# Attention and a Fourier-mixing block on one core: values and scores of batch 1 become two steps, and the block sums are scaled one step ahead

## The chip, the cores and the metric

The kernel runs on 1 core of one Trainium2 chip. The metric is the device time of one execution in microseconds (us), lower is better. The engines of the core are named as in the profile: PE is TensorE (its weight loads are PEld), DVE is VectorE, ACT is ScalarE, POOL is GpSimd, and SP is SyncE, which issues nearly all transfers here. Each engine runs its own list of instructions in order; the lists are tied together by semaphores.

## The reference, cut to what matters

There are 4 batches, 8 heads, 768 tokens and a head size of 64. A query sees the tokens closer than 16 to it and, beside them, one summary for each block of 32 tokens: the maximum of the block's keys and the mean of its values.

```python
k_sum = k.reshape(B, H, nb, block, D).max(axis=3)        # block = 32, nb = 24
v_sum = v.reshape(B, H, nb, block, D).mean(axis=3)
scores_l = scale * q @ k^T, where |i - j| < 16, else -1e9
scores_s = scale * q @ k_sum^T + log(block)
a = softmax(concat(scores_l, scores_s));  attn = a @ concat(v, v_sum)
x = attn as (batch, 768, 512)
u = x + real(fft(fft(x, axis=1), axis=2))
un = (u - mean) / sqrt(var + 1e-6)                        # over the last axis
out = u + maximum(un @ w_ch1, 0) @ w_ch2                  # 512 -> 2048 -> 512, float32
```

## The kernel before, in words

The kernel is one program for all four batches. Heads go in pairs g = 0 to 3, so a batch has four attention steps of two heads each. The work of one batch runs beside that of another: while batch b does its dense products, batch b+1 does its attention.

**The attention of batches 1 to 3** (`gen_attention`) is made of these parts for each pair:

- `prepare` turns keys and queries (for batch 1 on PE, 12 transposes `qk`, copied by ACT at L709; for later batches on DVE) and takes the block maxima of the keys (`km`, DVE, L714).
- `scores` makes 48 small matmuls `sc` (L773: 64 rows of weights, 32 columns), an exponential on ACT (L779) and a mask on DVE (`p`, recorded at the helper's line L567).
- `sum_scores` makes 4 matmuls `ss` with the block maxima (L789) and one exponential.
- `values` first makes one matmul `vs` (L796) that picks the pair's block sums out of the tile `vbs`, and scales them by a mask of ones and zeros, `half_of`, into the single SBUF tile `vs`: for batch 1 with one DVE multiply (L801), for batches 2 and 3 with two ACT activations (L799). Then it makes 48 small matmuls `av` with the values' windows (L810), 6 matmuls `av` with `vs` (L815), and DVE takes the reciprocal of the sums (`rec`, L819) and writes the result to `x`.
- `load_values` fetches the windows of a later pair into one of two buffers `vw`.

All of `qk`, `sc`, `ss`, `vs` and `av` take their PSUM tiles from one pool of four, in the order in which the program asks for them.

**The dense work** of a batch is: the Fourier transform along the tokens (`y`, L1209) and along the features (`mx`), normalising, transposes `unt` (L1287), then `gen_hidden` (h tiles, `hx`, `hy`, `hz`, L1313, seven products of two matmuls for each of the hidden tiles j = 0 to 7, four per half) and `gen_out` (`o`, L1359, for the first half of batch 0, else L1382). For batch 0 the weights arrive as float64 and are converted tile by tile (`make`, `convert`): raw `words` are loaded by SP, DVE makes two steps (L1058, L1059), ACT two (L1060, L1061), DVE three more (L1063, L1065 and a product), and for each W1 tile and the later W2 tiles four sums follow. A list `plan` says which tile is converted from which stage on. So in the first 235 us DVE converts weights beside everything else.

**What sets the order.** Python generators are stepped in turn by `drive`. Batch 1's attention is stepped in two calls: first beside batch 0's Fourier work, `drive((gen_fourier(0), 4, 600), (first(weights, 66), 12, 0), (first(attn, 5), 1, 0))`, and then beside batch 0's hidden and output work, `drive((most, 5, 0), (weights, 15, 0), (attn, 1, 0))`: in each round five dense steps, fifteen weight steps and one attention step. For batch 1 a pair took two attention steps: one with `values` of pair g-1, `scores` and `sum_scores` of pair g, and `load_values`; one with `prepare` of the next pair and its loads. Batches 2 and 3 had three yields between values and scores already. Within this program order a scheduler moves instructions on each engine by planned durations and dependencies; the result, the order of instructions as built, is fixed before the kernel runs and can be read. In that order batch 1's scores of a pair followed the values of the pair before directly for pairs 2 and 3.

Of the kernel before, what the change touches and what calls it, by code (L numbers as in the profile page):

```python
# [490 lines left out]
def _main_program(ctx, tc, q, k, v, moe_w_ch1, moe_w_ch2, out):  # L491
# [51 lines left out]
    vw_bufs = [cpool.tile([P, nb, D1], FP, name=f"vw{i}") for i in range(2)]  # L543
# [14 lines left out]
    def abank(shape, name):  # L558
        return psum.tile(shape, FP, tag="attn", bufs=4, name=name)

    def bank(shape, name):
        return psum.tile(shape, FP, tag="bank", bufs=4, name=name)
# [3 lines left out]
    def tt(out, in0, in1, op):  # L566
        return nc.vector.tensor_tensor(out=out, in0=in0, in1=in1, op=op).ins  # L567
# [28 lines left out]
    def room(name):  # L596
        return bpool.tile([P, NC * 2 * S], FP, tag="room", name=name)
# [52 lines left out]
    def load_values(b, g):  # L650
        if is_wide(b):
            load_wide_values(b, g)
            return
        load_narrow_values(b, g)
# [30 lines left out]
    def prepare(b, g, *which):  # L685
        qn, kn = (nat[b, g, n] for n in range(2))
        kt, km = kt_bufs[g % 2], km_bufs[g % 2]
        qt = apool.tile([P, S], FP, tag="qt", name=f"qt_{b}_{g}") if 0 in (which or (0,)) else None
        for n in which or (1, 0):
            src, dst = (kn, kt[:, W:W + S]) if n else (qn, qt)  # L690
            if (b, g) > (2, 0):
                with tc.issue_after(marks["dense"]):
                    nc.vector.transpose(out=dst, in_=src.rearrange("p m c -> p (m c)"))
                continue
            if is_wide(b):
                for h in range(2):
                    ps = bank([P, S2], f"qk_{b}_{g}_{h}")
                    for s in range(HT):
                        for e in range(2):
                            nc.tensor.matmul(ps[D * e:D * (e + 1), s:S2:HT], src[:, e, h, s, :], ident, start=True, stop=True)  # L700
                    nc.scalar.copy(out=dst[:, S2 * h:S2 * (h + 1)], in_=ps)
            else:
                for e in range(2):

                    ps = abank([P, S2], f"qk_{b}_{g}_{e}")
                    for j in range(NST // 2):
                        nc.tensor.transpose(ps[:, P * j:P * (j + 1)], src[:, e, j, :], ident)
                    for s in range(2):
                        nc.scalar.copy(out=dst[D * e:D * (e + 1), s:S:2], in_=ps[D * s:D * (s + 1)])  # L709
        if which == (0,):  # L710
            nat[b, g] = qt
            return
        with tc.issue_after(marks["fold", 0]) if (b, g) == (1, 0) else ExitStack():
            nc.vector.tensor_reduce(out=km[:, 0:nb], in_=kt[:, W:W + S].rearrange("p (n f) -> p n f", f=BLOCK),  # L714
                                    op=ALU.max, axis=AX.X)
        nat[b, g] = qt
# [72 lines left out]
                nc.tensor.matmul(ps[r:r + 32, :], km[rows, :], qt[rows, S2 * h:S2 * (h + 1)], start=True, stop=True)  # L789
        nc.scalar.activation(out=p, in_=ps, func=AF.Exp, scale=SC)  # L790

    def values(b, g, p, pm, x):
        vw = vw_bufs[g % 2]
        ps = abank([P, D], f"vs_{b}_{g}")
        vb, pick = sums[b, g]
        nc.tensor.matmul(ps, pick, vb, start=True, stop=True)  # L796
        if b > 1:
            for r in range(2):
                nc.scalar.activation(out=vs[:, r, 0:D], in_=ps, func=AF.Identity, scale=half_of[:, r:r + 1])  # L799
        else:  # L800
            tt(vs[:, :, 0:D], ps[:, None, :].to_broadcast([P, 2, D]),  # L801
               half_of[:, :, None].to_broadcast([P, 2, D]), ALU.mult)

        av = [abank([P, NST, D1], f"av_{b}_{g}_{r}") for r in range(2)]
        for t in range(NST):
            h = t // HT
            for j in range(4):
                for r in range(2):
                    rows, i = slice(64 * r, 64 * (r + 1)), 4 * t + j
                    nc.tensor.matmul(av[r][32 * j:32 * (j + 1), t, :], p[rows, h, i - NB2 * h, :], vw[rows, i, :],  # L810
                                     start=(t == 0), stop=False, skip_group_check=True)
        for t in range(HT):
            for r in range(2):
                rows = slice(64 * r, 64 * (r + 1))
                nc.tensor.matmul(av[r][:, t:t + HT + 1:HT, :], pm[rows, P * t:P * (t + 1)], vs[rows],  # L815
                                 start=False, stop=(t == HT - 1), skip_group_check=True)
        for r in range(2):
            rc = rec[:, b * NP + g, r]
            nc.vector.reciprocal(out=rc, in_=av[r][:, :, D])  # L819
            xo = x[:, 0, P * g + D * r:P * g + D * (r + 1)]  # L820
            xo = bass.AP(xo.tensor, xo.offset, [list(xo.ap[0]), [HT * DM + D * (1 - 2 * r), 2], [DM, HT], [1, D]])
            tt(xo, av[r].rearrange("p (h t) d -> p h t d", h=2)[:, :, :, 0:D],
               rc.rearrange("p (h t) -> p h t", h=2)[:, :, :, None].to_broadcast([P, 2, HT, D]), ALU.mult)
# [3 lines left out]
    def following(b, g, n):  # L827
        i = b * NP + g + n
        return divmod(i, NP) if i < B * NP else None
# [129 lines left out]
    def gen_attention(b):  # L959
        x = bpool.tile([P, NST, DM], FP, tag="x", bufs=2, name=f"x_{b}")  # L960
        x_of[b] = x
        held = None
        if b == 2:
            load(2, 1)
            load(2, 2)
        if b > 1:
            yield
            yield
            with tc.issue_after(marks["load"]):
                block_sums(b, 0)  # L970
            for _ in range(2):
                yield
        for g in range(NP + 1):
            n1, n3 = (following(b, g, n) for n in (1, 3))
            if held:
                values(b, g - 1, *held, x)
                if n1 and b > 1:
                    load_values(*n1)
            if g == NP and b > 1:
                turn_tiles(b, x)  # L980
                for _ in range(17):
                    yield
                rooms[b] = room(f"fold_{b}")
                steps = fold_batch(b, split_fold(b, rooms[b]))
                while True:
                    with tc.issue_after(marks["dense"]):
                        done = next(steps, steps) is steps
                    if done:
                        break
                    yield  # L990
            elif held and b > 1:
                yield
                yield
                yield
            if g < NP:
                held = scores(b, g)
                sum_scores(b, g, held[1])
            if g and n1 and b == 1:
                load_values(*n1)
            if g == 1 and b > 1:  # L1000
                block_sums(b, 1)
            if g == NP and b > 1:
                return
            yield
            if g == NP:
                return
            if b > 1:
                yield
                yield
            if n1:  # L1010
                prepare(*n1, *((1,) if b > 1 else ()))
            if b > 1:
                yield
                yield
                if n1:
                    prepare(*n1, 0)
            if n3 and not (b == 1 and n3 > (2, 0)):
                load(*n3)
            yield
            if b > 1:  # L1020
                yield
# [431 lines left out]
    def drive(*gens):  # L1453


        gens = list(gens)
        rounds = max(g[1] for g in gens)
        while gens:
            for s in range(rounds):
                for g in list(gens):  # L1460
                    gen, n, ahead = g
                    for _ in range(n * (s + 1) // rounds - n * s // rounds):
                        with tc.high_priority(ahead) if ahead else ExitStack():
                            done = next(gen, gens) is gens
                        if done:
                            gens.remove(g)
                            break

    def first(gen, n):
        for _, step in zip(range(n), gen):  # L1470
            yield

    weights = gen_weights()
# [16 lines left out]
        yield from gen_attention(1)  # L1490

    attn = second_attention()
    drive((gen_fourier(0), 4, 600), (first(weights, 66), 12, 0), (first(attn, 5), 1, 0))
    block_sums(1, 1)
    for b in range(B):

# [66 lines left out]
```

## Time and profile before

| what | value |
| --- | --- |
| median of 5 runs | 803.88 us (800.92 to 807.67) |
| the profiled execution | 812.89 us, its span 810.7 us |
| mean granted PE clock in the span | 0.980 |
| PE busy | 786.2 us (97%), 5914 matmuls |
| DVE busy | 496.2 us (61%) |
| ACT busy | 229.3 us (28%) |
| POOL busy | 61.5 us (8%) |
| chain that ended last | PE 90%, DVE 5%, ACT 3%, issue 2% |

The span runs from the first to the last instruction; 2.2 us of the profiled execution lie outside it. The profiled execution was 9.0 us longer than the median. Busy shares are averages over the whole span. By stretches, DVE is much fuller early on: 44.6 of 55 us between 145 and 200 us, 32.0 of 36 us between 200 and 236 us. The clock column of the windows is the clock that PE was granted, 1.00 being full. "issue" stands for time in which an engine waited for nothing that the profile shows.

### The profile page before, as it was taken

How to read it: one execution, taken by the hardware profiler on the slowest of the kernel's cores; microseconds unless marked ns; L12 is line 12 of the kernel's file. 1: busy time of each engine (PE TensorE's matmuls, PEld its weight loads, DVE VectorE, ACT ScalarE, POOL GpSimd, SP SyncE). 2: the span in 40 equal slices, each digit the busy share in tenths (PEclk: the TensorE clock that was granted, in tenths of full speed). 3: DMA queues.
4: the chain of work that ended last, by engine and by line, in shares of the span. 5: the costliest groups of instructions: out<-in, count | busy, mean ns of one | idle time of the engine just before them, and what ended most of it. 6: DMA issues, size and time to landing. Idle time of an engine off the chain costs nothing.

```text
span 810.7 us, 14470 instructions
## 1 busy us (share of the span) xinstructions
PE 786.2 (97%) x5914; PEld 572.9 (71%) x5914; DVE 496.2 (61%) x1115; ACT 229.3 (28%) x509; POOL 61.5 (8%) x103
## 2 busy tenths in 40 slices
PE   9988989999999999999999999999999999999997
PEld 6786655545569875588659875688659875786586
DVE  5789678688998836573476826464476723532352
ACT  3544448442745212210116212210116102001200
POOL 0012030000000012200030002300030000000000
PEclk9989699999999999999999999999999999999999
DMA  9999568499584457996344049820514044206001
GB/s 218 205 282 200 100 216 239 149 237 288 174 263 132 106 167 170 253 151 134 129 176 153 27 142 209 215 75 27 226 40 153 27 170 155 91 0 228 0 27 55
DMA packets 133354, 121.83 MB, mean 150 GB/s; under 512 B 94464, under 2 KB 114912, under 8 KB 133088
## 3 DMA queue, kind: packets, MB, share of 16 engines
q1 hardware_dynamic: 132016, 118.53, 53.0%
q0 software_dynamic: 576, 2.10, 0.7%
q8 instruction: 48, 0.79, 0.4%
q10 hardware_dynamic: 688, 0.20, 0.1%
q14 instruction: 26, 0.21, 0.1%
HBM read 97.22 MB, written 23.59 MB: 149 GB/s over the span
## 4 chain that ended last, share of the span: by engine, by line
PE 90%; DVE 5%; ACT 3%; issue 2%; DMA 0%; POOL 0%; SPq 0%; POOLq 0%
PE hx L1313 20%; PE ox L1382 18%; PE hz L1313 9%; PE oz L1382 9%; PE o L1359 5%; PE hy L1313 5%; PE oy L1382 4%; PE y L1209 3%; PE sc L773 3%; PE mx L1168 2%; PE av L810 2%; PE av L815 1%; PE unt L1287 1%; DVE p L567 1%; PE ss L789 1%
## 5 line engine op out<-in xcount | busy, mean ns | idle before, releaser
L1313 PE MATMUL hx<-u,w 128*128 128x384 f32 x512 | 189.7, 499 | 1.3 <-DVE h L567 0.7
L1313 PEld LDWEIGHTS hx<-u,w 128*128 128x128 f32 x512 | 96.6, 193 | 72.8 <-DVE h L567 4.3
L1313 PE MATMUL hz<-u,w 128*128 128x384 f32 x256 | 93.3, 487 | 0.0
L1382 PE MATMUL oz<-w,s 128*128 128x256 f32 x336 | 81.1, 379 | 0.0
L1382 PE MATMUL ox<-w,s 128*128 128x256 f32 x336 | 80.3, 380 | 0.0
L1382 PE MATMUL ox<-w,h 128*128 128x256 f32 x336 | 79.8, 381 | 0.0
L567 DVE TENSOR_TENSOR x<-ox,x 128x256 f32<-128x256 f32 x84 | 35.3, 423 | 67.7 <-PE ox L1382 67.5
L1313 PEld LDWEIGHTS hz<-u,w 128*128 128x128 f32 x256 | 48.8, 191 | 34.7 <-issue 0.8
L1382 PEld LDWEIGHTS ox<-w,h 128*128 128x128 f32 x336 | 63.0, 190 | 11.1 <-issue 1.2
L1382 PEld LDWEIGHTS ox<-w,s 128*128 128x128 f32 x336 | 63.0, 190 | 9.3 <-DVE x L567 0.8
L1382 PEld LDWEIGHTS oz<-w,s 128*128 128x128 f32 x336 | 63.4, 190 | 8.5
L1324 ACT COPY h<-hx 128x384 f32<-128x384 f32 x32 | 15.3, 479 | 189.7 <-PE hx L1313 189.7
L567 DVE TENSOR_TENSOR h<-hy,h 128x384 f32<-128x384 f32 x32 | 17.8, 558 | 48.6 <-PE hy L1313 48.5
L1313 PE MATMUL hy<-u,w 128*128 128x384 f32 x128 | 47.5, 493 | 0.0
L567 DVE TENSOR_TENSOR h<-hx,h 128x384 f32<-128x384 f32 x32 | 17.8, 556 | 45.5 <-PE hx L1313 45.5
L1359 PE MATMUL o<-w,h 128*128 128x512 f32 x96 | 42.1, 595 | 0.0
L1343 ACT ACTIVATE h<-hx 128x384 f32<-128x384 f32 x32 | 15.7, 491 | 88.5 <-PE hx L1313 88.4
L1382 PE MATMUL oy<-w,h 128*128 128x256 f32 x168 | 40.1, 380 | 0.0
L1313 PEld LDWEIGHTS hy<-u,w 128*128 128x128 f32 x128 | 24.4, 192 | 17.7 <-issue 1.2
L570 POOL TENSOR_TENSOR vb<-vb 96x512 f32<-96x512 f32 (+2 forms) x24 | 23.3, 971 | 174.4 <-DMA vb<-in_v_dram 107.7
L567 DVE TENSOR_TENSOR x<-oz,x 128x256 f32<-128x256 f32 x42 | 17.8, 423 | 29.7 <-PE oz L1382 29.4
L1382 PEld LDWEIGHTS oy<-w,h 128*128 128x128 f32 x168 | 31.8, 190 | 4.4
(164 smaller groups left out, 1106.3 us busy)
## 6 DMA issues: line engine op xcount, KB each, us to landing
w<-dw SPq DMA_DIRECT2D x44, 896.0 KB, 5.8
words<-in_moe_w_ch_dram SPq DMA_DIRECT2D x32, 512.0 KB, 5.6
dw<-w SPq DMA_DIRECT2D x12, 896.0 KB, 6.9
vw<-in_v_dram SPq DMA_DIRECT2D x47, 192.0 KB, 5.3
out_dram<-x SPq DMA_DIRECT2D x23, 256.0 KB, 2.0
vb<-in_v_dram SPq DMA_DIRECT2D x24, 192.0 KB, 6.0
kn<-in_k_dram SPq DMA_DIRECT2D x9, 384.0 KB, 4.6
qn<-in_q_dram SPq DMA_DIRECT2D x9, 384.0 KB, 5.8
```

What stands on the lines that cost most here:

```text
L567: return nc.vector.tensor_tensor(out=out, in0=in0, in1=in1, op=op).ins
L570: nc.gpsimd.tensor_tensor(out=out, in0=in0, in1=in1, op=op)
L773: nc.tensor.matmul(ps[h][r:r + 64, i, :], kt[rows, o:o + 64], qt[rows, o:o + BLOCK], start=True, stop=True)
L789: nc.tensor.matmul(ps[r:r + 32, :], km[rows, :], qt[rows, S2 * h:S2 * (h + 1)], start=True, stop=True)
L810: nc.tensor.matmul(av[r][32 * j:32 * (j + 1), t, :], p[rows, h, i - NB2 * h, :], vw[rows, i, :], start=(t == 0), stop=False, skip_group_ch ...
L1168: nc.tensor.matmul(out, y[:, g], table, start=False, stop=True, skip_group_check=True)
L1209: nc.tensor.matmul(y, fgs[b][par][:, st, P * g:P * (g + 1)], fs[par][:, g % 2, st, :], start=(st == 0), stop=(st == n - 1))
L1313: ins = nc.tensor.matmul(ps, w[:, a, kk, :], u[:, r, kk, :], start=start and kk == 0, stop=stop and kk == 1, skip_group_check=True)
L1324: nc.scalar.copy(out=c11, in_=X)
L1343: nc.scalar.activation(out=c21, in_=X, func=AF.Relu)
L1359: nc.tensor.matmul(ps, h[:, n, hf, P * t:P * (t + 1)], wt[2, b, j][:, 2 * hf:2 * hf + 2, :], start=(n, hf) == (0, 0), stop=(n, hf) == (NC ...
L1382: nc.tensor.matmul(ps, left[a][:, n, :], wt[2, b, j][:, r, :], start=start and n == 0, stop=stop and n == NC - 1, skip_group_check=True)
```

## The change

The first part of `values`, the matmul `vs` and its scaling, becomes a function of its own, `scale_sums`. It is called at the end of the step that prepares the next pair, for the pair whose values come next. For batch 1 there is now one yield between `values` of pair g-1 and `scores` of pair g, so a pair takes three attention steps in place of two: values; scores, sum scores and the loading of values' windows; preparation, scaling and loading. The first `drive` takes six attention steps in place of five, so that it ends behind the same preparation. In batches 2 and 3 only the place of `vs` and its scaling changes.

```diff
-    def values(b, g, p, pm, x):
-        vw = vw_bufs[g % 2]
+    def scale_sums(b, g):
         ps = abank([P, D], f"vs_{b}_{g}")
         vb, pick = sums[b, g]
         nc.tensor.matmul(ps, pick, vb, start=True, stop=True)
@@
             tt(vs[:, :, 0:D], ps[:, None, :].to_broadcast([P, 2, D]),
                half_of[:, :, None].to_broadcast([P, 2, D]), ALU.mult)
 
+    def values(b, g, p, pm, x):
+        vw = vw_bufs[g % 2]
         av = [abank([P, NST, D1], f"av_{b}_{g}_{r}") for r in range(2)]
@@
-            elif held and b > 1:
-                yield
-                yield
-                yield
+            elif held:
+                yield
+                if b > 1:
+                    yield
+                    yield
             if g < NP:
                 held = scores(b, g)
                 sum_scores(b, g, held[1])
@@
             if n1:
                 prepare(*n1, *((1,) if b > 1 else ()))
+            scale_sums(b, g)
             if b > 1:
                 yield
                 yield
@@
-    drive((gen_fourier(0), 4, 600), (first(weights, 66), 12, 0), (first(attn, 5), 1, 0))
+    drive((gen_fourier(0), 4, 600), (first(weights, 66), 12, 0), (first(attn, 6), 1, 0))
```

## The prediction

> **What bounds the kernel now.** I read the page's busy times first, then TensorE's list of waits, then its timeline around batch 1's attention, and last the windows by granted clock. Busy shares:
>
> ```profile
> PE 786.2 (97%) x5914; PEld 572.9 (71%) x5914; DVE 496.2 (61%) x1115; ACT 229.3 (28%) x509; POOL 61.5 (8%) x103
> ...
> q8 instruction: 48, 0.79, 0.4%
> ```
>
> TensorE works for 786.2 of 810.7 us, so a change that keeps its matmuls can win only from the 24.5 us of gaps and from time at a lower clock. The list of waits (what was waited for: total, times, longest) has one large entry, and nobody is named as its releaser:
>
> ```profile
> PE sc L773 <- issue: 8.3, 4, 3.3
> PE unt L1287 <- ACT big L1280: 2.1, 1, 2.1
> ```
>
> TensorE's timeline (start, length, what, in brackets the idle time before) shows where two of the four are, in batch 1:
>
> ```profile
> 110.30 0.94 PE L815 MATMUL av<-vs,p 64*128 64x130 f32 x12
> 111.17 1.59 PE L773 MATMUL sc<-qt,kt 64*64 64x32 f32 x94
> 116.08 0.24 PE L773 MATMUL sc<-qt,kt 64*64 64x32 f32 x2 [3.31 <-issue]
> ...
> 117.16 2.93 PE L1313 MATMUL hx<-u,w 128*128 128x384 f32 x4
> ...
> 121.36 1.45 PE L1313 MATMUL hx<-u,w 128*128 128x384 f32 x4
> ...
> 146.73 0.94 PE L773 MATMUL sc<-qt,kt 64*64 64x32 f32 x49
> 149.66 0.90 PE L773 MATMUL sc<-qt,kt 64*64 64x32 f32 x47 [1.99 <-issue]
> ```
>
> Each time values and scores run without dense work between, and TensorE stops in the middle of one tile's matmuls, 3.31 and 1.99 us. The first dense group afterwards takes 2.93 us where the same group takes 1.45. The windows (length, busy times, then clock, DMA share, GB/s) say why:
>
> ```profile
> 79.30:96.40 17.10, 16.12 (x204) 11.02 (x206) 9.75 (x17) 6.42 (x12) 0.00 (x0) 0.50 0.56 114
> ...
> 116.80:120.20 3.40, 3.40 (x9) 1.82 (x6) 3.32 (x3) 1.63 (x5) 3.24 (x3) 0.51 0.04 15
> ...
> 151.00:154.40 3.40, 3.40 (x12) 1.68 (x6) 2.78 (x6) 2.25 (x5) 0.00 (x0) 0.50 0.00 0
> ```
>
> After each of the two pauses the clock is halved for 3.4 us.
>
> **What the pauses are.** Queue q8 carries 0.79 MB in 48 packets, 16 KB each; TensorE has 11,958 records, 254 for each of the 47 steps between packets. I counted TensorE's instructions in the built order: a weight load and a matmul per pass (two passes for a matmul, one for a transpose, as the trace shows), and one per wait. The four pauses stand at 2758, 3267, 5317 and 5827; divided by 256 these leave 198, 195, 197, 195. So they stand at edges of 256-instruction blocks: TensorE had no next instruction. The packets that end the first two start at 113.83 and 147.47 us; TensorE goes on at 116.08 and 149.66, 2.2 us later both times. One block is in hand when the next is asked for (the crossing before the first pause was at 109.83). Values plus scores are about 430 instructions in 5 us and can run through a whole block in 2.9 us (109.83 to 112.76), while request and arrival took 4.0 + 2.2.
>
> [...]
>
> **The change, part by part.** (1) The built order now has dense work between values and scores of pairs 1/2 (after values: two h matmuls, 13 scores, 20 h, 35 scores) and 2/3 (21 matmuls of o). Counting block edges in it, batch 1's lie at instruction rows 511, 575, 644, 708, 777, 840, 904. Between 644 and 708 stand 22 dense rows of 0.65 us (1.29 us for x4), between 777 and 840 nine of 0.88: 14 and 8 us of cover against 6.2. Both pauses go: 5.3 us. After 1053 rows the counts are equal again, so batch 2's two pauses (1.66 and 1.36 us) stay.
>
> (2) The two half-clock windows follow the pauses: 2 x 3.41 x 1/2 = 3.4 us. The profiled execution took 812.89 us, 2.2 beyond its span and 9.0 over the median of 803.88. All low-clock stretches before 155 us (6.8, 17.1, 3.4, 3.4 long) cost 15.4 us; if the 9.0 are clock, 42% of this is left in timed runs. So I take 1.4 of 3.4, bounds 0 and 3.4.
>
> [...]
>
> (3) First pair: values of pair 0 and scores of pair 1 still follow directly (the rounds there hold no dense step), inside the half-clock stretch 79.3 to 96.4. Two h half-products that stood in it (1.65 us each instead of 0.81) now come later: up to 1.7 gained. But 48 scores in a row (2 x 2.77 us) have no dense work, and what ends the stretch isn't shown; the window with `ss` and `hy` ended it before. One more window of 3.4 costs 1.7, two cost 3.4 less the 1.7. Between +1.7 and -1.7 I take 0.
>
> (4) The same edge at row 575 now lies behind 13 rows of values and 48 of scores: 3.8 us at full clock. Request-to-arrival there was 1.05 + 2.2 = 3.3 in the trace: nothing. With the 4.0 of the first pause it would be 2.4. I take 0, the nearer row.
>
> (5) VectorE. From 97.0 to 158.2, when the second half of W2 tile 2 is ready, it is busy 47.95 us. In the built order TensorE needs that half as the sixth matmul of o_0. o_0 began at 154.2; from this go 8.7 (pauses and half clock) and 4.5 (values of pair 2 with 2.0 and scores of pair 3 with 2.5, which now come later), and five matmuls of 0.88 stand before the sixth: it is due at 145.4. Before that VectorE sheds 0.3 (vs), 1.3 (x of pair 2), 0.95 (mask of pair 3), and 1.5 (x of pair 0, now before 97): 43.9 us of work in 48.4. It waited in this stretch 2.8 us for the conversions' ACT half and 1.8 for h products, and both stay: 48.5. So the weights come just in time. Loss 0 to 5 us (if the waits for `rec` and `p`, 12.0 us, stay in part); I take 1, since most of those 12 were the pauses.
>
> (6) Scaling one step ahead: 24 products (0.25 us), 8 VectorE multiplies (0.28), 16 ACT activations (0.31), same number. Before, the 1.2 us of `av` matmuls covered the multiply; without cover it would be 0.3 per pair. In batches 2 and 3 TensorE waited for none: 0. In VectorE's queue vs_1 stands ahead of 24 conversions; its product is made at about 97, VectorE gets there at about 101: no wait. vs has one buffer, written after the last reader of the pair before. The pool's order of PSUM tiles is the same.
>
> (7) Moved loads: values windows of pairs 2 and 3 go behind two to four loads of raw weights on SP. They land 5.3 us after issue and are wanted 30 us later: 0. Raw weights come out from behind them, which can only help VectorE. Batch 1's last values move into h_5; 30 dense rows (19 us) follow before the Fourier products, and the fold on VectorE (236.7 to 249) keeps its place after h_7: 0.
>
> Sum: 5.3 + 1.4 + 0 - 1 = 5.7, so 803.88 - 5.7 = **798.2 us** (the profiled execution: 5.3 + 3.4 - 1 = 7.7, about 805).
>
> **Rivals.** *VectorE takes the gain* (0.17). For: 48.5 us of work and waits in 48.4. Against: before, the same tile was ready 2.2 us ahead. With the full 5 us lost, 802. *The pause only moves* to row 575 (0.10): 2.4 plus 0.7 of half clock, 801.3; against it is the short request there.
>
> *Slower* (0.18): VectorE is so late with the four halves of W2 tiles 2 and 3 that each stops TensorE 2 us and, as at 147.7, halves the clock for a window: 4 x (2.0 + 1.7) = 14.8 on top of 798.2, 813. It decides from three such stops (11.1, 809.3) on, i.e. with VectorE 6 us behind. Against it: matmuls of o_0_1 stand in the built order as filling between those of o_0_0.
>
> **How the numbers follow.** The forecast (both pauses gone, VectorE nearly in time) has 0.55; its own range is 793.5 (8.7 + 1.7 gained) to 799.8. Within 0.5% of 803.88, 799.9 to 807.9, about the least that a measurement of this kernel can tell from no change, lie the first two rivals, 0.27. Slower has 0.18. The range 793 to 807.5 holds forecast and both rivals and leaves out most of the slower case.
>
> **What would show it.** Right: TensorE's waits have `sc <- issue` only in batch 2, two times, about 3 us in all; the clock is 1.0 from about 100 us on. Wrong: a wait `o L1359 <- DVE w` or `<- DVE words`, a pause at `ss` near 92 us, a half-clock stretch that reaches past 100, or the h groups after scores still at 2.9 us.

## The result, and the profile after

The changed kernel takes 807.73 us (median; 803.04 to 813.52) where the kernel before took 805.61 in the same comparison: a ratio of 1.0026, 95% interval 1.0013 to 1.0038. In time that is 1.0 to 3.1 us lost, where 5.7 were forecast as gained. The pauses went, as forecast, and something else took more than they had cost.

The profiled execution took 802.8 us (span 800.9, clock 0.993), less than any of the timed runs; why is seen further down. Its busy shares:

```profile
PE 775.7 (97%) x5914; PEld 563.2 (70%) x5914; DVE 499.1 (62%) x1115; ACT 228.8 (29%) x509; POOL 61.4 (8%) x103
```

TensorE is idle for 800.9 - 775.7 = 25.2 us; before it was 24.5. So the gaps did not shrink, they changed owner. TensorE's list of waits after the change (total, times, longest) names the new owners:

```profile
PE vs L795 <- POOL vbs L570: 3.1, 2, 2.3
PE hx L1316 <- DVE h L567: 2.9, 3, 1.4
...
PE o L1362 <- DVE w L567: 0.6, 1, 0.6
```

`sc <- issue`, 8.3 us before, is gone altogether. In its place stand a wait for GpSimd that the kernel before did not have, and VectorE's `h` with 2.9 in place of 0.7. TensorE's timeline in batch 1 (start, length, what, idle time before) shows the first half of the story:

```profile
99.59 1.25 PE L811 MATMUL av<-vw,p 64*32 64x65 f32 x96
...
101.64 1.56 PE L1316 MATMUL hx<-u,w 128*128 128x384 f32 x4
103.12 0.65 PE L773 MATMUL sc<-qt,kt 64*64 64x32 f32 x26
...
125.04 2.85 PE L1316 MATMUL hx<-u,w 128*128 128x384 f32 x8 [1.40 <-DVE h L567]
...
144.97 4.56 PE L1362 MATMUL o<-w,h 128*128 128x512 f32 x10 [0.64 <-DVE w L567]
```

Dense work stands between values and scores, no matmul of scores waits, and every group `hx` of four takes 1.45 to 1.56 us, none 2.93. The window from 97 to 155 us is at the full clock (clock: third number from the right):

```profile
97.00:155.00 58.00, 54.71 (x461) 29.89 (x460) 47.96 (x94) 31.65 (x61) 6.24 (x6) 1.00 0.86 239
```

The second half of the story is in batches 2 and 3. GpSimd's timeline and TensorE's, after the change:

```profile
296.10 0.31 POOL L570 TENSOR_TENSOR vbs<-vb 96x64 f32<-96x64 f32 x1
```

```profile
292.74 1.45 PE L1316 MATMUL hx<-u,w 128*128 128x384 f32 x4
296.47 0.43 PE L795 MATMUL vs<-vbs,sel 96*128 96x64 f32 x2 [2.28 <-POOL vbs L570]
...
481.19 0.43 PE L795 MATMUL vs<-vbs,sel 96*128 96x64 f32 x2 [0.82 <-POOL vbs L570]
```

The matmul `vs` of pair 0 reads `vbs`, which GpSimd adds up from 290.87 on, from loads that have just landed. TensorE comes to `vs` 2.28 us too soon, and the hidden products that stand behind `vs` in its list, which need nothing from GpSimd, start only after it, at 296.74. The same places in the kernel before, TensorE and then GpSimd, batch 2 first:

```profile
302.93 2.74 PE L1313 MATMUL hx<-u,w 128*128 128x384 f32 x8
...
309.38 0.33 PE L796 MATMUL vs<-vbs,sel 96*128 96x64 f32 x2
...
496.44 0.33 PE L796 MATMUL vs<-vbs,sel 96*128 96x64 f32 x2
```

```profile
306.82 0.32 POOL L570 TENSOR_TENSOR vbs<-vb 96x64 f32<-96x64 f32 x1
...
491.89 0.32 POOL L570 TENSOR_TENSOR vbs<-vb 96x64 f32<-96x64 f32 x1
```

Before, `vbs` was ready at 307.14 and read at 309.38: a margin of 2.2 us. In batch 3 it was 496.44 - 492.21 = 4.2. The change moves `vs` ahead of four dense groups (the second half of the `hx` shown, and an `hy`, `hx` and `hz` behind it) that follow each other every 1.29 us, 5.2 us in all. 5.2 - 2.2 = 3.0 and 5.2 - 4.2 = 1.0 us of waiting were to be read off the trace of before; 2.28 and 0.82 came.

### The profile page after: what moved, and what is told of

Read it like the earlier page. It is cut to its first block, busy times and chain, and to the rows that moved or that the text cites. A ratio compares the mean times of both kernels' runs of the same rounds, so it can differ in the third digit from the quotient of the medians.

```text
span 800.9 us, 14469 instructions
## 1 busy us (share of the span) xinstructions
PE 775.7 (97%) x5914; PEld 563.2 (70%) x5914; DVE 499.1 (62%) x1115; ACT 228.8 (29%) x509; POOL 61.4 (8%) x103
## 4 chain that ended last, share of the span: by engine, by line
PE 82%; DVE 12%; ACT 2%; POOL 1%; DMA 1%; issue 1%; ACTq 0%; SPq 0%; DVEq 0%; POOLq 0%
PE ox L1385 18%; PE hx L1316 17%; PE oz L1385 9%; PE hz L1316 9%; PE oy L1385 5%; PE o L1362 4%; PE hy L1316 4%; PE y L1212 4%; PE mx L1171 2%; DVE w L567 2%; PE sc L773 2%; PE unt L1290 1%; PE av L811 1%; POOL vb L570 1%; DVE x L567 1%; PE av L816 1%
## 5 line engine op out<-in xcount | busy, mean ns | idle before, releaser
L1316 PE MATMUL hx<-u,w 128*128 128x384 f32 x512 | 186.2, 491 | 4.4 <-DVE h L567 2.9
L1316 PEld LDWEIGHTS hx<-u,w 128*128 128x128 f32 x512 | 94.8, 190 | 72.3 <-DVE h L567 5.3
```

The source lines that it names most:

```text
L1316: ins = nc.tensor.matmul(ps, w[:, a, kk, :], u[:, r, kk, :], start=start and kk == 0, stop=stop and kk == 1, skip_group_check=True)
```

## Experiments

Theory: the pauses in batch 1 cost what the prediction said, and the early `vs` of pair 0 in batches 2 and 3 costs more, by its wait for GpSimd and by half clock behind the wait, as it stood behind the two pauses of before (3.31 and 1.99 us, 3.4 us at about 0.50 after each). Rivals: the pauses never cost much in timed runs; or VectorE in batch 1 takes the gain. Kernels run together stood on one chip, beside the same runs of the kernel before: the four of the first heading, the four of the two headings after it, and late scaling (second time), its form with early sums and the mask on GpSimd; the last run stood alone on a fourth chip.

### Taking the change apart

The kernel before, profiled again:

> The kernel before, unchanged, for a second profile. The profile on which the prediction rests was 9.0 us above the median. Theory A (the pauses at block edges are part of every execution): four waits sc <- issue again, at the same four instruction counts, 2 us or more in batch 1 each, 6 to 9 us in all; less time at half clock, so a span near 803. Theory B (the pauses belonged to that one execution): less than 3 us of sc <- issue, and then the forecast's first term of 5.3 us was never there to gain.

It took 802.73 us, span 800.7, clock 0.991; the first profile had 0.980. TensorE's timeline:

```profile
109.53 0.24 PE L773 MATMUL sc<-qt,kt 64*64 64x32 f32 x2 [2.53 <-issue]
...
142.85 0.90 PE L773 MATMUL sc<-qt,kt 64*64 64x32 f32 x47 [1.89 <-issue]
```

The pauses stand in the same places, behind the same 94 and 49 matmuls, and the clock is 0.50 for 3.41 us after each, from 110.61 and from 144.75. 2.53 + 1.89 + 3.4 = 7.8 us are there in an execution below the median too. Three waits `sc <- issue` came, not four: batch 2 has one, of 1.06 us. The clock near the first pair is another matter: the stretch at 0.50 that was 17.1 us long in the first profile, from 79.3 us on, is not there at all; the window from 74 to 97 us is at 1.00.

This execution also has `vs` of batch 2, with less room than the first, TensorE's row and GpSimd's:

```profile
302.61 0.33 PE L796 MATMUL vs<-vbs,sel 96*128 96x64 f32 x2
```

```profile
301.26 0.38 POOL L570 TENSOR_TENSOR vbs<-vb 96x64 f32<-96x64 f32 x1
```

The margin is 302.61 - 301.64 = 1.0 us, and in batch 3 it is 3.0. By this trace, moving `vs` 5.2 us ahead would cost 4.2 and 2.2 us.

The changed kernel with scaling put back in batches 2 and 3:

```diff
             if held:
+                if b > 1:
+                    scale_sums(b, g - 1)
                 values(b, g - 1, *held, x)
@@
-            scale_sums(b, g)
+            if b == 1:
+                scale_sums(b, g)
```

> The changed kernel with the block sums of batches 2 and 3 scaled directly before the values again; batch 1 as changed. Theory A (the gain was paid out to GpSimd's block sums, for which the early vs now waits: 2.28 and 0.82 us, and 0.70 us behind the second): these waits go, 3.8 us less than the changed kernel, ratio to before 0.998. Theory B (these waits only take the place of batch 2's pauses of 1.66 and 1.36 us, which come back): 1.0 us less, ratio 1.0015.

Ratio to the kernel before **0.9922**, interval 0.9892 to 0.9952 (799.34 against 806.74 us). A second time, on another chip, it was 0.9927 (0.9894 to 0.9959):

> The changed kernel with batches 2 and 3 scaled directly before their values, once more, to stand beside the two others. If the wait for GpSimd's block sums is the whole of what the changed kernel lost: ratio to the kernel before 0.990 to 0.996 again (0.9922 the first time), no wait of vs for GpSimd, two waits of hx for VectorE's h, together about 2.2 us. Rival (the first ratio was a lucky draw and the scaling's place is worth little): 0.998 or more.

The first execution's waits of TensorE:

```profile
PE hx L1319 <- DVE h L567: 2.2, 2, 1.4
...
PE sc L773 <- issue: 1.8, 2, 0.9
...
PE o L1365 <- DVE w L567: 0.6, 1, 0.6
```

No `vs` waits for GpSimd. The forecast gain (0.7%) is there, and the whole sign of the result hangs on where `vs` is made in two batches. Against the changed kernel that is some 8 us, far more than the 3.8 that had been expected from the waits in the one profile after (ratio 0.998); why is seen under the next heading. The two halves of the change alone, first the yield with scaling directly before the values everywhere:

```diff
             if held:
+                scale_sums(b, g - 1)
                 values(b, g - 1, *held, x)
@@
-            scale_sums(b, g)
```

> Only the new step between values and scores of batch 1; scaling directly before the values in all batches. Theory A: no pauses in batch 1, no wait for GpSimd; the same waits of TensorE for VectorE as in the changed kernel (about 3.5 us); ratio 0.998. If scaling ahead helps batch 1 (its vs on VectorE is covered less here), it is slower than late23 by 0.3 us a pair, ratio 0.999. Theory B as for late23: 1.0015.

Ratio 0.9963 (0.9931 to 0.9994). It is faster, but less than the kernel above; the intervals overlap, and the difference (batch 1's early scaling, which can have moved other work too) was not followed up. Then the scaling one step ahead without the yield:

```diff
-            elif held:
+            elif held and b > 1:
+                yield
+                yield
                 yield
-                if b > 1:
-                    yield
-                    yield
@@
-    drive((gen_fourier(0), 4, 600), (first(weights, 66), 12, 0), (first(attn, 6), 1, 0))
+    drive((gen_fourier(0), 4, 600), (first(weights, 66), 12, 0), (first(attn, 5), 1, 0))
```

> Only the scaling one step ahead, in all batches; values and scores of batch 1 in one step as before. Theory A: the pauses of batch 1 stand where they stood (about 5.3 us) and the waits for GpSimd are there (3.1 and 0.7 us): 3.8 us slower than before, ratio 1.005. If scaling ahead costs nothing: 1.000.

Ratio 1.0088 (1.0060 to 1.0116), 813.02 us, more than the 1.005 expected. It has both evils, the pauses of before and the waits of after:

```profile
PE sc L773 <- issue: 6.5, 2, 4.0
PE vs L795 <- POOL vbs L570: 4.8, 2, 4.0
```

and its `vs` of batch 2 is followed by 6.83 us at half clock (window: length, busy times, then clock):

```profile
306.43:313.26 6.83, 6.48 (x12) 3.75 (x13) 0.46 (x1) 1.00 (x3) 1.10 (x2) 0.50 0.73 206
```

### Which `vs`, and what it waits for

The changed kernel with only pair 0 of batches 2 and 3 scaled late:

```diff
             if held:
+                if b > 1 and g == 1:
+                    scale_sums(b, 0)
                 values(b, g - 1, *held, x)
@@
-            scale_sums(b, g)
+            if b == 1 or g:
+                scale_sums(b, g)
```

> The changed kernel, but in batches 2 and 3 the sums of pair 0 alone are scaled directly before the values; pairs 1 to 3 one step ahead. Theory A (the loss is TensorE's wait for GpSimd's sums of the first four heads, which only pair 0 can meet first): all of late23's gain, ratio 0.992, no vs <- POOL. Theory B (scaling ahead in batches 2 and 3 costs by its place in ACT's and TensorE's queues, in every pair): a quarter of the gain, ratio 1.000.

Ratio 0.9946 (0.9917 to 0.9975). Two of the 12 `vs` carry the loss. The other remedy leaves every `vs` early and has GpSimd's data early too: the block sums are asked for two steps sooner, and no longer held back behind the marked load.

```diff
         if b > 1:
-            yield
-            yield
-            with tc.issue_after(marks["load"]):
-                block_sums(b, 0)
-            for _ in range(2):
+            block_sums(b, 0)
+            for _ in range(4):
                 yield
```

> The changed kernel with the first block sums of batches 2 and 3 asked for two steps earlier and without the constraint to come after the last weight load; scaling stays one step ahead everywhere. Theory A: GpSimd starts some 4 us sooner, the wait of 2.3 us or more goes, ratio 0.992 to 0.996. Theory B (place of the scaling): ratio stays near 1.003.

Ratio 0.9960 (0.9936 to 0.9985), no `vs` waits for GpSimd, which is done 15 us earlier:

```profile
280.83 0.32 POOL L570 TENSOR_TENSOR vbs<-vb 96x64 f32<-96x64 f32 x1
```

With `vs` where the change puts it and its data there in time, the loss turns into a gain. So it is the data, not the place as such. The changed kernel itself ran beside these two:

> The changed kernel again, for a second profile and for a measurement beside the others. Theory A: ratio 1.003; the profile so far was at the fast end of its runs (802.8 against a median of 807.7), so this one should show a longer wait vs <- POOL (4 us, as in scale_only) and a half-clock stretch after it in batch 2 or 3. If the profile again shows 3.1 us and no half clock there, 5 us of the 8 lost remain unexplained.

Ratio 1.0036 (1.0009 to 1.0064). This profiled execution took 806.51 us, close to the median, and it shows the full price. TensorE's timeline, and the windows behind the two waits:

```profile
296.64 0.47 PE L795 MATMUL vs<-vbs,sel 96*128 96x64 f32 x2 [4.04 <-POOL vbs L570]
296.91 2.87 PE L1316 MATMUL hx<-u,w 128*128 128x384 f32 x4
...
483.31 0.43 PE L795 MATMUL vs<-vbs,sel 96*128 96x64 f32 x2 [2.05 <-POOL vbs L570]
```

```profile
296.90:300.31 3.41, 3.41 (x8) 1.90 (x8) 0.00 (x0) 1.00 (x3) 0.00 (x0) 0.50 0.74 187
...
484.64:488.05 3.41, 3.41 (x7) 1.87 (x6) 0.00 (x0) 0.48 (x1) 0.00 (x0) 0.50 0.95 304
```

6.1 us of waiting and 2 x 3.41 x 1/2 = 3.4 of half clock: 9.5 us. The waits of 4.04 and 2.05 us are close to the 4.2 and 2.2 that the second trace of before gives. In the first profile it was 3.1 and no half clock, 6.4 us less; a half-clock stretch near 50 us, 6.83 us long there and 3.41 here, takes 1.7 of that back, and the spans differ by 3.7. Between 3.1 and 9.5 lie the 7.3 us that the runs of this chip give (1.0036 against 0.9946, 0.9% of 805).

### The block edges

The kernel before with 32 tiny matmuls more in the warm-up, 128 instructions of TensorE, so that every block edge falls half a block earlier in the work:

```diff
         nc.tensor.matmul(ps, zeros[:, 512:640], zeros[:, 0:512], start=True, stop=True)
+    for i in range(32):
+        nc.tensor.matmul(ps[0:64, 0:32], zeros[:, 512:576], zeros[:, 0:32], start=True, stop=True)
```

> The kernel before with 32 more tiny matmuls among the warm-up ones (128 more TensorE instructions at the start, results not used). If the pauses stand at edges of 256-instruction blocks, all edges move 32 rows earlier: the first pause of batch 1 moves to sc after 15 of its 48 rows (30 of 96 matmuls, where it stood after 94); the second goes, since from the edge at row 809 to that at 873 there are now some 7 us of work; batch 2's two go too. If the pauses have another cause, they stay after 94 and 49 matmuls.

806.13 us, one run. All pauses of `sc` left the places that they had, as blocks of 256 ask for. The one expected in a new place of batch 1 didn't come: the transfer of its block began at 109.49, the edge was at about 113, in time. But two other stops came:

```profile
PE hz L1313 <- ACT h L1332: 3.2, 1, 3.2
PE qk L700 <- issue: 2.1, 1, 2.1
```

The first is of a kind the prediction did not have; TensorE goes on at 122.11, and the clock is 0.50 for 3.41 us from 121.54 us on. The second, at 28.34 us in batch 0, is a pause of the old kind in a new place. Counted in the traces, 2753, 3265, 5313 and 5825 weight loads, matmuls and waits of TensorE begin before the four pauses of before, and 705 before this one: divided by 256, all five leave 193. Behind it the clock is 0.50 for 10.24 us, from 29.38 us on. So the edges are shown as the cause of the pauses, and shifting them bought nothing in this run: a pause came back at an edge elsewhere.

### VectorE in batch 1, and a better kernel

Late scaling and early block sums together:

> Batches 2 and 3 scaled directly before their values, and besides it the block sums of pair 0 asked for two steps earlier. Theory (the early block sums only matter through the wait of vs): nothing left to win, the same ratio as without them, 0.990 to 0.996. Rival (the earlier loads and sums have a price of their own, which would explain why 0.996 was measured with the early sums alone against 0.9922 and 0.9946 with late scaling): about 0.3% more than without them, 0.995 to 0.998.

799.24 us against 804.74, ratio 0.9918 (0.9881 to 0.9954): the same as late scaling alone on that chip (0.9927), nothing left to win there. These two are the best whole kernels of the study. What they have left in batch 1 is VectorE's lateness. On top of late scaling, batch 1's mask goes from VectorE to GpSimd:

```diff
-            tt(p[:, h], p[:, h], near[:, h], ALU.mult)
+            (gtt if b == 1 else tt)(p[:, h], p[:, h], near[:, h], ALU.mult)
```

> Late scaling in batches 2 and 3, and batch 1's mask multiplication of p given from VectorE to GpSimd (8 instructions of about 0.48 us each on VectorE). Theory A (VectorE is late for h and w in batch 1 because it is full there): it sheds about 3.8 us before 158 us, the waits of hx for VectorE's h (2.2 us) and of o for w (0.6 us) go, ratio about 0.3% lower than without it, 0.987 to 0.992. Rival B (VectorE's steps grow while GpSimd works, as 0.68 to 1.75 us beside the block sums, and av now waits for GpSimd's slower mask): no gain or a loss, 0.993 to 1.0, with waits of av or hx of 2 us or more that name GpSimd or VectorE.

810.87 us, ratio 1.0060 (1.0026 to 1.0094), 10.9 us worse than the kernel that it was made from. Rival B holds, and beyond its numbers. VectorE's timeline in this kernel, one kind of instruction at two times, then GpSimd's at the second time:

```profile
65.99 1.68 DVE L567 TENSOR_TENSOR w<-w 128x256 f32<-128x256 f32 x4
...
129.18 5.05 DVE L567 TENSOR_TENSOR w<-w 128x256 f32<-128x256 f32 x4
```

```profile
128.82 2.31 POOL L570 TENSOR_TENSOR p<-p,near 128x384 f32<-128x384 f32 x2 [7.54 <-ACT p L779]
...
131.10 2.84 POOL L570 TENSOR_TENSOR vb<-vb,vb 96x512 f32<-96x512 f32 x2
```

Four additions take 1.68 us while GpSimd rests, and 5.05 us while it runs instructions of 1.2 to 1.4 us each back to back: about one addition is finished for each GpSimd instruction. TensorE then waits 3.02 us for `h`, until 134.75, and the clock from 134.8 to 138.2 is 0.58. The other damage was done earlier: the mask of the first pair now stands ahead of the block sums in GpSimd's queue, so these start at 78.26 instead of 67.09, on top of the normalising, and TensorE's transposes wait 5.43 us for VectorE's `big` in place of 2.04. Not all of that need be the mask: with pair 0 alone scaled late, and the mask on VectorE, the same wait is 3.58.

This suggests that the block sums in batch 1 make VectorE late even without the mask. The growth is not new with the change; the kernel before has it too, beside the same block sums:

```profile
118.16 1.75 DVE L1063 SCALAR_TENSOR_TENSOR words<-words 128x512 int32<-128x512 int32 x1
119.83 1.21 DVE L1065 SCALAR_TENSOR_TENSOR words<-words 128x512 f32<-128x512 uint32 x1
```

There TensorE had just stood 3.31 us at its pause, and no `hx` of batch 1 waited for VectorE. The last run is late scaling with early block sums, and leaves out seven of the eight additions for pairs 2 and 3 of batch 1, so that the values of these pairs lack most of their block sums:

```diff
-        gtt(raw[0], raw[0], raw[1], ADD)
-        gtt(raw[2], raw[2], raw[3], ADD)
-        gtt(raw[0], raw[0], raw[2], ADD)
-        while f > 2:
+        adds = ((0, 1), (2, 3), (0, 2)) if (b, gg) != (1, 1) else ()
+        for i, j in adds:
+            gtt(raw[i], raw[i], raw[j], ADD)
+        while adds and f > 2:
```

> Late scaling and early block sums as before, and of the 8 additions of batch 1's block sums for pairs 2 and 3 only the last is left (7 on GpSimd are left out, so the values of those two pairs in batch 1 lack most of their block sums; the loads stay). In the kernel with them GpSimd is busy with them from 111.3 to 118 us, and three VectorE steps in that time take 1.50, 1.56 and 1.21 us where such steps take 0.42 to 0.69 elsewhere: 2.5 us. Theory A (this collision makes VectorE late in batch 1): the three steps go back to 0.4 to 0.7 us, the waits of hx and o for VectorE (1.39 and 0.66 us) go or shrink to under half, ratio 0.2 to 0.4% lower than 0.9918, that is 0.988 to 0.990. Rival B (VectorE is late because it is full, and TensorE is ahead of it anyway): the steps get shorter, but VectorE spends the time waiting for ScalarE's half of the conversion, the waits of hx and o stay within 0.5 us, ratio 0.991 to 0.993.

Ratio 0.9907 (0.9872 to 0.9941), between the two theories' ranges, and its interval covers both. The waits decide what the time can't:

```profile
PE o L1362 <- DVE w L567: 0.6, 1, 0.6
PE hx L1316 <- DVE h L567: 0.5, 1, 0.5
```

The three steps are back at 0.42 to 0.69 us, and `hx` waits 0.5 us in place of 2.2: most of that wait was the collision with GpSimd, as theory A has it. The wait of `o` for the weights stays at 0.6: that one does not come from the collision. That it is VectorE's load itself, as B has it, is likely but not shown.

## Why the prediction was wrong, step by step

(1) **Pauses**, 5.3 us: right. They stood at edges of blocks and went with dense work between; 5.3 and 4.4 us in two executions of before, none in two of after.

(2) **Half clock behind them**, taken as 1.4 of 3.4: too low. The second execution of before, at 802.73 us, has both windows, so there it was the whole 3.4. The prediction spread the 9.0 us by which the first profile exceeded the median over all its half-clock stretches; nearly all of them fit in one, the 17.1 us near the first pair (8.5 us), which the second profile does not have. An estimate from the timed runs agrees: span times (1 - clock), the time lost to a lower clock, is on average 8.7 and 8.3 us in the kernel before and 5.5 both times in late scaling, on the two chips where they ran together.

(3), (4), (7) **First pair, row 575, moved loads**, 0 each: neither `ss` nor `sc` of batch 1 waits for instructions in the kernel after, and no load is named. But the stretch at half clock near the first pair moves by far more than the 1.7 us allowed: it is 17.1 us long or absent in the two executions of before, 3.4 in both of after, 10.2 with the yield alone. That is up to 8.5 us between executions of one kernel; what sets it is not shown.

(5) **VectorE**, loss 1, bounds 0 and 5: mis-sized within its bounds. In batch 1 of the profile after, TensorE waits 0.79 and 1.40 us for `h` and 0.64 for `w`: 2.8 us. Before, it waited there for neither (the 0.7 for `h` of before stands in batch 3). The prediction followed only the weights that `o` reads, and for these its 1 was near. The `h` that `hx` waits for was not in its sum. The steps that grow beside GpSimd (1.75 and 1.21 us in two rows of before, shown above) did not change the sum: they stood in the trace of before, and so in the 47.95 us of VectorE's work that it used.

(6) **Scaling one step ahead**, "In batches 2 and 3 TensorE waited for none: 0". This is the step that failed. That TensorE waited for none says only that there was a margin, not how large it was. The prediction followed what reads `vs` (the multiply, the activations, the buffer) and not what `vs` reads. The margin, 2.2 us and 4.2 (1.0 and 3.0 in the second execution), stood in the trace of before, and `vs` was moved 5.2 us ahead. The step cost 3.1 us in one profile and 6.1 + 3.4 in the other.

The sum with the sizes measured, without (6): 5.3 + 3.4 - 2.8 = 5.9 us, 0.73% of 804; late scaling measured 0.78 and 0.73%. With (6), 3.1 to 9.5, it runs from 2.8 gained to 3.6 lost; measured was a loss of 1.0 to 3.1. By the estimate used under (2), the changed kernel wins back almost none of the half clock (7.8 us on average against 8.3 in the kernel before beside it), and the rest of its span is 3.5 us longer (798.1 against 794.5). The slower rival had a stop of 2 us with half clock behind it. The runs showed one (2.05 us, then 3.41 us at 0.50), but at the wait for GpSimd: the stops of batch 1 for VectorE's `h` and `w` were 0.64 to 1.40 us, and the window from 97 to 155 us is at 1.00.

Batch 2's two pauses were to stay and did not: 3.0 us in the first profile of before, 1.06 in the second, none after. Where `vs` of batch 2 waits for GpSimd (both executions of after, and scaling alone) there is none; in the kernels without that wait and with the edges in place there are one or two, of 0.26 to 1.66 us. This suggests that the wait gives the missing block time to arrive, and so pays back a little of (6); no run tests it.

## What to carry to other kernels

When an instruction is moved ahead in an engine's list, list what it reads, find in the trace when each of these was ready, and subtract the time by which it moves from the margin; "nothing waited before" is not a margin. What is left over is charged to what stands behind it, here the hidden products behind `vs`, and most of the stops of 1.89 to 4.04 us counted here were followed by 3.41 us or more at 0.50, at least another 1.7 us; the one of 2.28 in batch 2 after the change was not. Before giving work to an idle GpSimd, look at what VectorE does at that moment: four additions that took 1.68 us while it rested took 5.05 while it ran.

## What the runs showed of the hardware that was not expected

**Short stops and the clock.** Stops of 2.53 and 1.89 us (the kernel before, second profile) and of 4.04 and 2.05 (the changed kernel, second profile) were each followed by 3.41 us at 0.50, and so was one of 1.46 in batch 2 of late scaling (second time); one of 4.00 (scaling alone) was followed by 6.83. Others, of 1.36 and 1.66 us in batch 2 of before and of 2.28 after the change (both first profiles), were followed by 1.00. What decides whether a stop of about 2 us costs a window is not shown.

**VectorE beside GpSimd.** Where the two met, VectorE instructions often grew by up to the length of one GpSimd instruction: from 0.42 to 1.26 on average in the four additions above, and even steps of 128x3 elements, in the kernel with the mask on GpSimd, beside additions of 1.27 us (3.82 for three):

```profile
78.31 1.23 DVE L1263 TENSOR_SCALAR stat<-both 128x3 f32<-128x3 f32 x1
79.45 0.15 DVE L1271 SCALAR_TENSOR_TENSOR norm<-norm 128x3 f32<-128x3 f32 x1
79.58 1.18 DVE L1266 TENSOR_SCALAR norm<-stat 128x3 int32<-128x3 int32 x1
```

The steps of L1263 and L1266 take 0.15 to 0.21 us in late scaling (second time), with the mask on VectorE. Which steps grow and which don't is not shown: of these 128x3 steps two grew by about 1 us, and the step at 79.45 went through at 0.15 between the two.
